# The first weight load of a two-branch decode kernel, cut into eight transfers by partition

## The chip, the cores and the metric

The kernel runs on one core of a Trainium2 chip; the other cores are idle. The metric is the device time of one execution in microseconds (us). Before the change three runs gave a median of 1324.18 us, with a lowest of 1323.75 and a highest of 1324.31.

## The reference

Two attention branches, A and B, work on the same input and are mixed by a gate. Each branch projects the input to one query per head and batch entry, scores it against a cached key tensor, takes the softmax and applies it to a cached value tensor, then projects the result out.

```python
# B=2 batch entries, Sq=1, D=512; Hq=Hkv=32 heads, Sk=4096 tokens, Dh=128; all float32
def branch(x, k_cache, v_cache, wq, wo):
    q = (x @ wq).reshape(B, Sq, Hq, Dh).transpose(0, 2, 1, 3)
    scores = einsum("bhqd,bhkd->bhqk", q, k_cache) * (Dh ** -0.5)
    p = softmax(scores, axis=-1)
    o = einsum("bhqk,bhkd->bhqd", p, v_cache)
    return o.transpose(0, 2, 1, 3).reshape(B, Sq, Hq * Dh) @ wo

g = sigmoid((A_x * gate_w).sum(-1, keepdims=True))
result = g * branch(A_x, ...A...) + (1 - g) * branch(A_x, ...B...)
```

Each cache is 2 x 32 x 4096 x 128 floats, 134 MB; there are four of them, and four weight matrices of 8.4 MB each. All of it is read once: 570.43 MB.

## The kernel before

The work is cut into 32 units: branch, group of four heads, batch entry. A unit has a key tile and a value tile of 128 partitions x 16384 floats, that is 64 KB on each partition and 8.39 MB in all (8192 KB). On-chip memory has room for three such tiles: two for keys (`kt[0]`, `kt[1]`) and one (`vt`) that holds the values, and ahead of them the query weights of the branches, one after the other.

All large loads are issued by SyncE (SP in the profile) on one queue, in the order of the code. That order is: A's query weights into `vt` (`load_wq("A")`, L218 to L221), unit 0's keys into `kt[0]` in two halves (L225), B's query weights into `vt` (L486), unit 1's keys into `kt[1]`, unit 0's values into `vt`, and from there keys and values of the following units in turn (L508 to L512), then the two output weights. A load that overwrites a tile waits on SyncE until the tile's last reader is done: B's query weights wait for `queries("A")`, the values wait for the matmuls that read the values before (`v_free`), the keys wait for VectorE's scores of two units ago (`k_free`).

At the start TensorE turns the input into columns (`cols`, L287 to L289). It then runs `projections()` (L327), a loop of two rounds, one for each branch, whose body is written once: take 16 from the semaphore `wq_landed`, which the weight load raises by 16 when it has landed; take one from `cleared`, which VectorE raises when it has zeroed the accumulators `qa`; then 64 matmuls of the 512 x 4096 weights. `take` (L94) waits for a semaphore and lowers it again, so that both rounds can wait for the same count. `queries(n)` (L341) then has ScalarE copy the sums into `vt` and VectorE transpose them into `qcol`; when VectorE's last reading of `vt` is done, SyncE may issue the next load of `vt`.

The weights lie on the partitions as rows of the matrix: partition p holds the four rows 4p to 4p+3, which are 64 KB in a row in memory on either side.

From there VectorE multiplies every key tile with the queries and sums it up (L392 and L395, the scores), ScalarE takes the exponentials, and TensorE multiplies them with the values (L371). At the end the sums of all units are projected out.

## Time and profile before

| | |
|---|---|
| median of the runs | 1324.18 us (1323.75 to 1324.31) |
| profiled execution: span from first to last instruction | 1322.3 us |
| bytes read | 570.43 MB |
| VectorE busy | 1165.3 us |
| TensorE busy | 331.7 us |
| ScalarE busy | 100.7 us |
| issue of A's query weights on SyncE | 0.96 us after the span's start, 0.40 us long |
| issue to landing of that load | 21.8 us |
| first projection's matmuls on TensorE | from 23.06 us, 9.49 us long |

The profiled execution's own time is its span of 1322.3 us; it has no other clock, and the runs stand 1.9 us above it. In the profile an engine's name with a q behind it is that engine's sequencer (SPq is SyncE's, which issues loads). A stretch of the trace is given as start and end in us from the span's start, with the busy time of every engine in it, how many instructions, the clock granted to TensorE (PEclk), the share of the 16 DMA engines' time that packets took, and the bytes moved per second. Both of the last are booked at the moment in which a packet begins, so that a short stretch can show more than its share.

### The profile page before, as it was taken

Reading aid. Unit: us, or ns where it says so; the run is one execution under the profiler, and the core shown is the slowest. Engines: PE = TensorE matmul, PEld = TensorE weight load, DVE = VectorE, ACT = ScalarE, POOL = GpSimd, SP = SyncE. Lnnn points to the kernel's source line nnn. Section 1 sums busy time; section 2 is a strip of 40 time slices with the busy share of each in tenths; the row PEclk is TensorE's granted clock in tenths of the full one; section 3 lists DMA queues with packets and bytes.
Section 4 is the critical chain, followed back from the end, with each engine's and each line's share of the span. In section 5 each row is a group of like instructions: output and inputs, shape, how many; then the busy total and the mean of one; then the engine's idle time right before and its main releaser. Section 6 shows DMA issues by size and latency. Waiting matters only on the chain. (4 is left out here: it accounts for less than half of the span.)

```text
span 1322.3 us, 6216 instructions
## 1 busy us (share of the span) xinstructions
PE 331.7 (25%) x2382; PEld 90.3 (7%) x2382; DVE 1165.3 (88%) x316; ACT 100.7 (8%) x328; POOL 0.7 (0%) x6
## 2 busy tenths in 40 slices
PE   3112222211222221122222122222212322311256
PEld 0000000000000000000000000000000000000011
DVE  1978999999999999999999999999999999999961
ACT  0000100001010000101000010100001010000100
POOL 0000000000000000000000000000000000000000
PEclk9566666556666655666665666666556666555678
DMA  9999999999999999999999999999999999999998
GB/s 404 453 412 443 442 416 442 442 416 442 442 418 442 440 436 424 442 440 418 442 440 418 442 442 416 442 442 424 436 442 436 422 442 440 418 442 442 417 442 352
DMA packets 10820, 570.51 MB, mean 431 GB/s; under 512 B 1207, under 2 KB 1467, under 8 KB 1726
## 3 DMA queue, kind: packets, MB, share of 16 engines
q1 hardware_dynamic: 10804, 570.43, 99.6%
q8 instruction: 3, 0.05, 0.0%
q14 instruction: 3, 0.02, 0.0%
q10 hardware_dynamic: 10, 0.01, 0.0%
HBM read 570.43 MB, written 0.00 MB: 431 GB/s over the span
## 5 line engine op out<-in xcount | busy, mean ns | idle before, releaser
L392 DVE TENSOR_TENSOR kt<-kt,q 128x16384 f32<-128x16384 f32 x31 | 534.0, 17226 | 71.3 <-DVEq L97 71.3
L395 DVE TENSOR_REDUCE sc<-kt 128x128 f32<-128x16384 f32 x31 | 533.8, 17220 | 1.1
L371 PE MATMUL vp<-vt,pr 128*32 128x512 f32 x1984 | 283.1, 734 | 915.5 <-PEq L97 915.5
L371 PEld LDWEIGHTS vp<-vt,pr 128*32 128x32 f32 x1984 | 77.9, 132 | 1120.7 <-issue 1120.7
L367 ACT ACTIVATE pr<-sc,nm 32x128 f32<-32x128 f32 x128 | 50.9, 398 | 108.1 <-ACTq L97 102.8
L430 ACT ACTIVATE pr<-nil 128x512 f32<-128x512 f32 x31 | 19.3, 623 | 456.8 <-ACTq L97 456.8
L451 ACT ACTIVATE vs<-vp,slot 128x128 f32 x15 | 5.5, 368 | 448.1 <-ACTq L97 448.1
L337 PE MATMUL qa<-vt,cols 128*2 128x512 f32 x128 | 18.4, 739 | 39.9 <-PEq L97 39.9
L367 ACT ACTIVATION_READ_ACCUMULATOR pr<-sc,nm (+1 forms) x128 | 23.5, 184 | 0.0
L416 DVE SCALAR_TENSOR_TENSOR vs<-vp,slot,vs 128x128 f32 x45 | 15.8, 351 | 8.6 <-DVEq L97 7.6
L599 DVE COPY kt<-qa 2x128 f32<-2x128 f32 x1 | 0.3, 278 | 23.8 <-PE qa L481 23.8
L352 DVE STREAM_TRANSPOSE vt<-vt 128x1024 f32<-128x1024 f32 x2 | 2.4, 1224 | 17.1 <-ACT vt L348 17.1
L498 DVE TENSOR_REDUCE sc<-kt 128x64 f32<-128x8192 f32 x2 | 17.4, 8686 | 0.1
L496 DVE TENSOR_TENSOR kt<-kt,q 128x8192 f32<-128x8192 f32 x2 | 17.4, 8688 | 0.0
L455 ACT ACTIVATE vp<-nil 128x512 f32<-128x512 f32 x15 | 9.0, 600 | 99.2 <-ACTq L97 99.2
L544 DVE SCALAR_TENSOR_TENSOR vs<-vp,slot,vs 128x128 f32<-128x128 f32 x3 | 1.1, 351 | 12.9 <-ACT vs L542 12.8
L371 PE MATMUL vp<-kt,pr 128*32 128x512 f32 x64 | 9.0, 724 | 10.9 <-DMA kt<-in_B_v_cache_dram 10.9
L466 PE MATMUL most<-vt,kt 128*2 128x512 f32 x64 | 9.6, 765 | 6.5 <-DMA vt<-in_A_wo_dram 6.5
L400 DVE TENSOR_REDUCE rm<-sc 128x1 f32<-128x128 f32 x31 | 8.7, 281 | 2.3
L406 DVE STREAM_TRANSPOSE q<-qsel 128x128 f32<-128x128 f32 x30 | 9.3, 311 | 1.0
L289 DVE COPY cols<-bank 128x8 f32<-128x8 f32 x1 | 0.2, 167 | 10.0 <-PE bank L287 10.0
L401 DVE STREAM_TRANSPOSE across<-rm 128x32 f32<-128x32 f32 x31 | 6.6, 212 | 1.1
(73 smaller groups left out, 60.4 us busy)
## 6 DMA issues: line engine op xcount, KB each, us to landing
kt<-in_A_k_cache_dram SPq DMA_DIRECT2D x2, 4096.0 KB, 35.6
kt<-in_B_wo_dram SPq DMA_DIRECT2D x1, 4096.0 KB, 33.1
kt<-in_B_wo_dram SPq DMA_DIRECT2D x1, 2048.0 KB, 37.6
kt<-in_B_wo_dram SPq DMA_DIRECT2D x1, 1024.0 KB, 39.5
kt<-in_B_wo_dram SPq DMA_DIRECT2D x1, 512.0 KB, 40.3
vt<-in_A_v_cache_dram SPq DMA_DIRECT2D x16, 28.5
kt<-in_B_k_cache_dram SPq DMA_DIRECT2D x16, 42.6
kt<-in_B_wo_dram SPq DMA_DIRECT2D x1, 256.0 KB, 40.4
```

Of the source, the lines that this page charges most:

```text
L337: last = nc.tensor.matmul(t[h * QT:h * QT + B], cols[:, c], blocks[:, c, i, h], start=c == 0, stop=c == KC - 1)
L367: do(lambda x: x.activation(padded[h, :, b, j * VC:(j + 1) * VC], s[h].rearrange("p (c a) -> p c a", a=VC), AF.Exp, bias=m[h], accum_out=l ...
L371: return x.matmul(vp[c % STRIPS * QT:(c % STRIPS + 1) * QT], padded[:, c].rearrange("p b m -> p (b m)"), t[:, c * VC:(c + 1) * VC].rearran ...
L392: at = D_.do(lambda x: x.tensor_tensor(kt[o], kt[o], q[:, None, :].to_broadcast([P, NS, DH]), op=ALU.mult), after)
L395: at = D_.do(lambda x: x.tensor_reduce(sc[o], kt[o], axis=AX.X, op=ALU.add), at)
L406: return D_.do(lambda x: x.transpose(q, qsel[:, 0].to_broadcast([P, DH // QT, QT])), at)
L416: at = D_.do(lambda x: x.scalar_tensor_tensor(vs[:, g], vp[:, a * DH:(a + 1) * DH], slot[:, a:a + 1], vs[:, g], op0=ALU.mult, op1=ALU.add) ...
L430: return A_.do(lambda x: x.activation(padded[:, :, b], nil[:, :, None].to_broadcast([P, NVC, G * VC]), AF.Copy))
L455: A_.do(lambda x: x.activation(vp, nil.to_broadcast([P, VC * DH]), AF.Copy))
L466: put("pe", lambda x: x.matmul(most[s * QT:s * QT + B], on[:, k, r], wo[n][:, r], start=n == "A" and r < STRIPS, stop=n == "B" and r >= EA ...
L496: put("dve", lambda x: x.tensor_tensor(t, t, q[:, None, :].to_broadcast([P, NS // 2, DH]), op=ALU.mult), [r_q], [r])
L498: put("dve", lambda x: x.tensor_reduce(sc[0][:, h * NS // 2:(h + 1) * NS // 2], t, axis=AX.X, op=ALU.add), [r], [R()])
```

## The change

A's query weights go out as eight transfers instead of one. Transfer r holds the partitions r, r+8, r+16 and so on to r+120: 16 partitions of 64 KB, 1 MB in all. The first seven raise a new semaphore, `wq_first`, and the last one raises `wq_landed`. TensorE waits for 7 x 16 on `wq_first` once, ahead of the loop over the branches; inside the loop it takes 16 from `wq_landed` as before. B's query weights still go out as one transfer.

```diff
+EACH = 8
...
+        wq_first = sem("wq_first")
...
         def load_wq(n):
             S.before("sp", [], [r_vt])
-            nc.sync.dma_start(vt.rearrange("p r d -> p (r d)"),
-                              ins[n + "_wq"].rearrange("(p c) f -> p (c f)", c=KC)).then_inc(wq_landed, 16)
+            to, src = vt.rearrange("p r d -> p (r d)"), ins[n + "_wq"].rearrange("(p c) f -> p (c f)", c=KC)
+            if n == "B":
+                nc.sync.dma_start(to, src).then_inc(wq_landed, 16)
+                return
+            for r in range(EACH):
+                nc.sync.dma_start(to[r::EACH], src[r::EACH]).then_inc(wq_first if r < EACH - 1 else wq_landed, 16)
...
         def projections():
-            S.wait("pe", r_cols.writers)
+            S.wait("pe", [*r_cols.writers, (wq_first, 16 * (EACH - 1))])
```

On SyncE, at the start of the program, the loads stood like this before (a row names the line, the tile that is written, the tensor that is read, and the shape; what it waits for stands in brackets):

```order
L220 DMA vt<-in_A_wq_dram 128x16384
L106 DMA kt_85<-in_A_k_cache_dram 128x8192 x2
L106 UNCONDITIONAL_BRANCH
L220 DMA vt<-in_B_wq_dram 128x16384 [waits done_dve]
L231 DMA kt_86<-in_A_k_cache_dram 128x16384 [waits landed_x,done_pool,landed_y,done_act,done_pe]
```

and now like this:

```order
L227 DMA vt<-in_A_wq_dram 16x16384 x8
L107 DMA kt_85<-in_A_k_cache_dram 128x8192 x2
L107 UNCONDITIONAL_BRANCH
L224 DMA vt<-in_B_wq_dram 128x16384 [waits done_dve]
L237 DMA kt_86<-in_A_k_cache_dram 128x16384 [waits landed_x,done_pool,landed_y,done_act,done_pe]
```

One row has become eight, ahead of the two halves of unit 0's keys; what follows is as it was. On TensorE, around the start of the projections, the program now reads:

```order
L293 MATMUL bank<-kt_86 128x3 [waits landed_y,landed_x,done_pool]
L293 MATMUL bank<-kt_86 128x3 x3
L310 MATMUL bank<-kt_86 128x2 [waits done_dve]
L335 UNCONDITIONAL_BRANCH [waits wq_first]
L343 MATMUL qa_89<-vt,cols 2x512 [waits wq_landed,cleared]
```

The wait for `wq_first` stands at the loop's entry, where there was none; the matmuls behind it waited for `wq_landed` and `cleared` before as well.

## The prediction

> **What bounds the kernel now.** I read the page's summary first, for who is busy and what was moved.

> ```profile
> span 1322.3 us, 6216 instructions
> PE 331.7 (25%) x2382; PEld 90.3 (7%) x2382; DVE 1165.3 (88%) x316; ACT 100.7 (8%) x328; POOL 0.7 (0%) x6
> DMA  9999999999999999999999999999999999999998
> q1 hardware_dynamic: 10804, 570.43, 99.6%
> ```

> VectorE is busy for 88% and would be the suspect, but the DMA row shows 9 from the first slice on, and the queue that SyncE feeds (q1) fills 99.6% of the time of 16 DMA engines. Then stretches of the trace, each of 19.3 us at first, then two long ones:

> ```profile
> core 0: us, PE busy (x) PEld busy (x) DVE busy (x) ACT busy (x) POOL busy (x), PEclk, DMA share, GB/s
> 5.00:21.80 16.80, 1.20 (x6) 1.05 (x6) 4.91 (x19) 0.17 (x1) 0.00 (x0) 1.00 1.01 437
> 21.80:41.10 19.30, 9.49 (x64) 1.76 (x64) 6.85 (x7) 1.08 (x2) 0.00 (x0) 0.84 1.01 435
> 41.10:60.40 19.30, 0.00 (x0) 0.00 (x0) 19.27 (x3) 0.00 (x0) 0.00 (x0) 0.50 1.00 435
> 60.40:79.70 19.30, 8.90 (x64) 1.68 (x64) 13.83 (x9) 3.04 (x10) 0.00 (x0) 0.77 1.00 435
> 99.00:699.00 600.00, 144.09 (x1024) 39.72 (x1024) 558.25 (x135) 46.28 (x152) 0.00 (x0) 0.62 1.00 435
> 699.00:1279.00 580.00, 139.00 (x960) 38.17 (x960) 539.80 (x125) 46.65 (x157) 0.00 (x0) 0.61 1.00 434
> ```

> The rate is the same 434 to 437 GB/s everywhere, with VectorE idle or full, TensorE idle or at work. A load of 8.39 MB takes 8.39 / 0.435 = 19.3 us, and loads follow one another with no gap. So the kernel is one stream of loads; the chain of waits confirms its end:

> ```profile
> 1276.98 39.55 DMA kt<-in_B_wo_dram
> 1316.53 0.04 issue
> ```

> The last load ends at 1316.5 us, and 5.8 us of matmuls and storing follow. The stream has no idle time that could swallow a delay: **what A's query weights cost more or less in the stream moves the end by the same amount**, as long as the next loads are queued in time. The sums below are made on the span of 1322.3 us; the median of the runs, 1324.18, is 1.9 us above it, and I carry that over.

> **How one load looks now.** Packets are booked when they begin, so thin stretches show them as rounds:

> ```profile
> 1.80:2.60 0.80, 0.00 (x0) 0.00 (x0) 0.00 (x0) 0.80 (x1) 0.00 (x0) 1.00 3.88 1316
> 2.60:5.00 2.40, 0.00 (x0) 0.00 (x0) 0.00 (x0) 0.46 (x1) 0.00 (x0) 1.00 0.00 0
> 5.00:5.60 0.60, 0.00 (x0) 0.00 (x0) 0.00 (x0) 0.00 (x0) 0.00 (x0) 1.00 4.03 1748
> 5.60:7.40 1.80, 0.00 (x0) 0.00 (x0) 0.00 (x0) 0.00 (x0) 0.00 (x0) 1.00 0.00 0
> 7.40:8.00 0.60, 0.00 (x0) 0.00 (x0) 0.00 (x0) 0.00 (x0) 0.00 (x0) 1.00 4.04 1751
> ```

> Each busy stretch is one round of A's weights: 1748 GB/s x 0.60 us = 1.05 MB, sixteen packets of 64 KB, one partition's row for each DMA engine. The rounds begin at 5.0 and 7.4: 2.4 us a round (19.3 / 8 = 2.41), eight rounds for the load. The first takes longer: it begins at 1.8 to 2.6 and the second at 5.0, about 3.0 us, so the start costs about 0.6 us once.

> **The change, part by part.** *The same bytes in the same number of packets:* eight transfers of sixteen rows of 64 KB are again eight rounds of sixteen packets, if each of the 16 engines takes one row of each transfer. *More issues:* SyncE's part of the time line is

> ```profile
> 0.96 0.40 SPq L220 DMA_DIRECT2D vt<-in_A_wq_dram  x1
> 1.41 0.89 SPq L106 DMA_DIRECT2D kt<-in_A_k_cache_dram  x2
> 35.34 0.33 SPq L220 DMA_DIRECT2D vt<-in_B_wq_dram  x1
> 35.86 0.33 SPq L231 DMA_DIRECT2D kt<-in_A_k_cache_dram  x1
> 74.47 0.33 SPq L239 DMA_DIRECT2D vt<-in_A_v_cache_dram  x1
> ```

> At 0.44 us each (0.89 / 2), seven more end 3.1 us later, and unit 0's keys are issued by about 5.4 us instead of 2.3. The engines then still have most of A's weights to move (till 21.8), and a transfer of one round lasts 2.4 us against an issue of 0.44: nothing runs dry. Cost nothing, covered by the queue; without that cover it would be 3.1 us. *Seven more completion marks on each engine:* the key load that goes out in two halves ran at 435 GB/s (21.80 to 41.10), as did the undivided one after it, so one mark more is under the resolution of 0.1 us; seven are under 0.7, and I take 0.1. *The wait for `wq_first`:* behind it on TensorE stand only the projections, which need the whole of the weights anyway. It ends with the seventh transfer, ahead of the eighth or with it: nothing.

> *Where the rows land.* This is the term that decides. Between 5.0 and 21.8 us each engine moves 64 KB in 2.4 us, 27 GB/s, and sixteen make the 435 that no stretch exceeds. A ceiling that stays the same whatever the compute engines do is a fixed width of the path: either of the 16 movers, or of the entrances by which they write into on-chip memory. The trace holds only loads over all 128 partitions, so no row tells which. If it is the movers, it doesn't matter which partitions a transfer holds. If it is the entrances, a transfer over all partitions must be dealt out so that each mover has an entrance to itself, since it reaches the full rate; a transfer of every eighth partition leaves no such choice. All sixteen rows in flight have the same place within a group of eight partitions, and all movers go on to the next place together, so they would keep meeting at some entrances while others stand empty, through all eight transfers.

> Bounds: below, the change wins back the slow start, 0.6 us for the long first round and 0.6 for the spread of the first starts, -1.2. Above, all sixteen rows through one entrance would be sixteen times 2.4 us a round, 8 x 15 x 2.41 = +289. The least sharing that there can be throughout is two movers to an entrance: a round then takes 2 x 2.41 and the load 8 x 2.41 = **19.3 us more**. I take that, the sharing nearest to the rows, with up to 0.6 us back, since the slow start overlaps with a slower round: +19.0.

> [...]

> *What is late next.* A's weights land around 42 us instead of 22.8 (0.96 + 21.8, below); every load behind them starts later by the same. The matmuls and the copies:

> ```profile
> vt<-in_A_wq_dram SPq DMA_DIRECT2D x1, 21.8
> 10.39 0.61 PE L287 MATMUL bank<-kt 3*128 3x3 f32 x4 [10.39 <-DMA kt<-in_gate_w_dram]
> 23.06 9.49 PE L337 MATMUL qa<-vt,cols 128*2 128x512 f32 x64 [10.68 <-PEq L97]
> 35.12 0.20 DVE L353 COPY qcol<-vt 128x64 f32<-128x64 f32 x1
> ```

> From landing to the issue of B's weights it is 35.34 - 22.8 = 12.5 us, and in that time unit 0's keys (19.3 us of stream) keep the engines busy until 41.1: 5.8 us to spare. Both shift together, so the spare time stays; the stream gets no hole, and nothing is caught up either. The small loads of the input and the gate, for which TensorE waits until 10.39, go through engines that also carry the weights and may come up to twice as late, near 20 us; the columns are needed at 42. Sum: 1322.3 + 19.0 = 1341.3 of span, 1324.2 + 19.0 = **1343.2 us**, 1.4% slower.

> **The rivals.**

> *The movers are the limit* (not slower). For it: the one rate in all rows, which fits this as well; every row that was read is of 128 partitions. Against it: nothing in the trace. Then the load stays at eight rounds of 2.41 us: 1324.2 + 0.1 for the marks, less up to 1.2 at the start, 1323.1 to 1324.3.

> *The change doesn't spread a transfer over all movers:* rows are dealt out by the partition they go to, so a transfer of every eighth partition uses half of the movers, two rows each; the first four transfers feed one half, the last four the other. Then the second half starts four issues later, 4 x 0.44 = 1.8 us, and each mover still carries eight rows: at most +1.8, 1326.0, within what can't be told. For it: full rate with 128 partitions needs some such order. Against it: the rows can't show it.

> *A faster start:* sixteen rows are prepared sooner than 128, so all movers begin at once. It can give the 1.2 us of the bound, 1323.0, which is no measurable gain; more than that isn't there to be had, because the stream has no other gap.

> *Sharing by four:* sixteen rows on four entrances, a round of 4 x 2.41: 8 x 3 x 2.41 = +57.8, 1382. Against it: distances of eight should reach more places than that.

> *Sharing only in part,* since the movers drift apart: half of the 19.3, 1334. Against it: the rounds above stay 2.4 us apart with starts inside 0.6 us, so the movers hardly drift.

> **How the numbers follow.** Less than 0.2% (2.6 us) can't be told from no change here. From the rows alone movers and entrances fit equally; I lean to the entrances because a rate that is the same to 1% in stretches with quite different reads, and with any load on the compute engines, is more easily a width of the memory's side. Chances: sharing by two 0.76, movers the limit 0.11, dealt by partition 0.06, sharing by four 0.03, in part 0.02, a start that wins over 2.6 us 0.02. Slower: 0.76 + 0.03 + 0.02 = 0.81; within 0.2%: 0.11 + 0.06 = 0.17; faster 0.02. The likeliest case's own range is 1341 (the start's 1.2 us won back, and a little drift) to 1347 (a tenth of 38.6 us lost where two streams meet). It holds about 0.7 by itself, so the range has to reach to the cases without a change: 1323 to 1347, which leaves out about 0.1.

> **What would show it.** Right: in stretches of the changed trace A's weights run at about 217 GB/s until about 41 us, with rounds 4.8 us apart; landing after the issue of the first transfer about 40 us; the first projection's matmuls begin near 42 us; B's weights are issued near 54.5; from there 435 GB/s in every stretch and the span 19 us longer; the matmuls and the scores as long as before. Wrong: rounds 2.4 us apart as now and the projection at about 23 us (the movers are the limit); half of the packets in the first rounds, the others 1.8 us later (dealt by partition); 110 GB/s (sharing by four). A hole in the stream between unit 0's keys and B's weights would make the step on the spare time wrong, and the sum would grow by the hole.

## The result, and the profile after

The changed kernel takes 1344.98 us (median; 1344.79 to 1345.37), the kernel before 1324.18: a ratio of 1.0158, with a 95% interval of 1.0147 to 1.0170. It is 20.8 us slower; the forecast was 19.0 us slower, 1343.2 us.

The page of the changed kernel, the lines that answer to those shown of before:

```profile
span 1343.1 us, 6223 instructions
PE 331.8 (25%) x2382; PEld 90.9 (7%) x2382; DVE 1165.2 (87%) x316; ACT 100.7 (8%) x328; POOL 0.7 (0%) x6
DMA  9899999999999999999999999999999999999998
GB/s 219 344 437 438 435 437 437 435 437 433 422 429 437 437 435 437 437 435 437 437 420 429 435 437 437 435 437 437 435 437 433 422 429 437 437 435 437 438 435 349
q1 hardware_dynamic: 10916, 570.43, 99.6%
```

The engines do the same work in the same time, the queue is as full as it was (99.6%), but in the first of 40 slices the DMA engines move 219 GB/s, with a busy share of 9 tenths. They are occupied and deliver half. The cause lies in the first 1.3 slices, where A's weights are loaded. There, in stretches that each hold the beginnings of one round of packets (up to 1.7 us behind the start of the stretch):

```profile
core 0: us, PE busy (x) PEld busy (x) DVE busy (x) ACT busy (x) POOL busy (x), PEclk, DMA share, GB/s
1.60:6.60 5.00, 0.00 (x0) 0.00 (x0) 0.00 (x0) 1.28 (x1) 0.08 (x1) 1.00 0.97 211
6.60:11.70 5.10, 1.20 (x6) 1.05 (x6) 1.81 (x8) 0.17 (x1) 0.00 (x0) 1.00 1.01 206
...
16.80:21.90 5.10, 0.00 (x0) 0.00 (x0) 0.00 (x0) 0.00 (x0) 0.00 (x0) 1.00 1.00 206
21.90:26.80 4.90, 0.00 (x0) 0.00 (x0) 0.00 (x0) 0.00 (x0) 0.00 (x0) 1.00 1.01 214
26.80:31.90 5.10, 0.00 (x0) 0.00 (x0) 0.00 (x0) 0.00 (x0) 0.00 (x0) 1.00 1.00 206
...
37.00:42.10 5.10, 0.00 (x0) 0.00 (x0) 0.00 (x0) 0.00 (x0) 0.00 (x0) 1.00 1.01 206
42.10:61.45 19.35, 8.83 (x64) 1.71 (x64) 6.36 (x7) 1.08 (x2) 0.00 (x0) 0.92 0.98 413
61.45:80.80 19.35, 0.00 (x0) 0.00 (x0) 19.32 (x3) 0.00 (x0) 0.00 (x0) 0.50 1.05 454
```

A round of sixteen 64 KB rows (206 GB/s x 5.10 us = 1.05 MB) takes 5.1 us where it took 2.4. One round, the fifth, takes 4.9. Unit 0's keys begin behind the eighth round, at 42.4 us, and their first round still overlaps the last slow packets, which end at 43.4. The mean of 413 and 454 GB/s in the last two stretches is the old rate within 0.4%: packets are booked when they begin, so what the one lacks the other has. Thin stretches show the first two rounds of the keys and the first of B's weights, before:

```profile
21.90:22.50 0.60, 0.00 (x0) 0.00 (x0) 0.00 (x0) 0.00 (x0) 0.00 (x0) 1.00 2.04 874
23.10:23.70 0.60, 0.60 (x4) 0.06 (x8) 0.00 (x0) 0.00 (x0) 0.00 (x0) 1.00 2.02 874
41.20:41.90 0.70, 0.00 (x0) 0.00 (x0) 0.70 (x1) 0.00 (x0) 0.00 (x0) 0.50 3.47 1498
```

and after:

```profile
42.40:43.50 1.10, 0.00 (x0) 0.00 (x0) 0.00 (x0) 0.00 (x0) 0.00 (x0) 1.00 1.52 477
44.30:44.90 0.60, 0.34 (x4) 0.14 (x8) 0.00 (x0) 0.00 (x0) 0.00 (x0) 1.00 2.02 874
62.50:63.00 0.50, 0.00 (x0) 0.00 (x0) 0.50 (x1) 0.00 (x0) 0.00 (x0) 0.50 4.85 2097
```

The trace has the start of every packet, and the mean of a round's sixteen starts tells how the delay grows (us):

| | before | after | later by |
|---|---|---|---|
| first round of A's weights | 2.20 | 2.61 | 0.4 |
| second round of A's weights | 5.26 | 7.46 | 2.2 |
| first round of unit 0's keys | 22.18 | 42.98 | 20.8 |
| second round of unit 0's keys | 23.38 | 44.63 | 21.2 |
| first round of B's weights | 41.54 | 62.78 | 21.2 |

What follows is shifted:

```profile
0.96 5.04 SPq L227 DMA_DIRECT2D vt<-in_A_wq_dram  x8
6.05 1.06 SPq L107 DMA_DIRECT2D kt<-in_A_k_cache_dram  x2
56.18 0.33 SPq L224 DMA_DIRECT2D vt<-in_B_wq_dram  x1
...
44.56 8.83 PE L343 MATMUL qa<-vt,cols 128*2 128x512 f32 x64 [33.74 <-PEq L98]
...
1297.91 39.43 DMA kt<-in_B_wo_dram
```

The last load ends 20.8 us later (1337.3 against 1316.5). That is 0.4 us less than the delay of B's weights in the table, which is within the 0.6 us by which single runs of either kernel differ; the 1280 us of stream between passed the delay on. B's weights are issued 20.8 us later too (56.18 against 35.34), but that is a coincidence: the first projection begins 21.5 us later (44.56 against 23.06) and in this profile is 0.7 us shorter (8.83 against 9.49).

### The profile page after: what moved, and what is told of

It is laid out like the page before. It is cut to its first block, busy times and chain, and to the rows that moved or that the text cites. A ratio compares the mean times of both kernels' runs of the same rounds, so it can differ in the third digit from the quotient of the medians.

```text
span 1343.1 us, 6223 instructions
## 1 busy us (share of the span) xinstructions
PE 331.8 (25%) x2382; PEld 90.9 (7%) x2382; DVE 1165.2 (87%) x316; ACT 100.7 (8%) x328; POOL 0.7 (0%) x6
## 2 busy tenths in 40 slices
DMA packets 10932, 570.51 MB, mean 425 GB/s; under 512 B 1319, under 2 KB 1579, under 8 KB 1838
## 3 DMA queue, kind: packets, MB, share of 16 engines
q1 hardware_dynamic: 10916, 570.43, 99.6%
HBM read 570.43 MB, written 0.00 MB: 425 GB/s over the span
## 5 line engine op out<-in xcount | busy, mean ns | idle before, releaser
L436 ACT ACTIVATE pr<-nil 128x512 f32<-128x512 f32 x31 | 19.3, 624 | 460.1 <-ACTq L98 460.1
L550 DVE SCALAR_TENSOR_TENSOR vs<-vp,slot,vs 128x128 f32<-128x128 f32 x3 | 1.1, 351 | 12.5 <-ACT vs L548 12.4
L343 PEld LDWEIGHTS qa<-vt,cols 128*2 128x2 f32 x128 | 3.4, 94 | 76.4 <-issue 76.4
```

The lines of the kernel that those rows point to most:

```text
L343: last = nc.tensor.matmul(t[h * QT:h * QT + B], cols[:, c], blocks[:, c, i, h], start=c == 0, stop=c == KC - 1)
L436: return A_.do(lambda x: x.activation(padded[:, :, b], nil[:, :, None].to_broadcast([P, NVC, G * VC]), AF.Copy))
```

## The experiments

All but the last vary only how A's weights are cut, in `load_wq`; the last cuts B's weights as well. The theory is that of the prediction: rows in flight together meet at a limited number of entrances into on-chip memory. The runs below test it by their own times; none shows an entrance. Where the text counts entrances, sixteen, eight or four, that is an estimate from the rates: 435 GB/s over all partitions, 206 in the change, 112 with sixteen neighbours, at one mover to an entrance in the first case.

### Eight transfers over all partitions

```diff
-                nc.sync.dma_start(to[r::EACH], src[r::EACH])...
+                at = slice(r * NS * DH // EACH, (r + 1) * NS * DH // EACH)
+                nc.sync.dma_start(to[:, at], src[:, at])...
```

> A's query weights go out as eight transfers again, but each over all 128 partitions with an eighth of the columns (8 KB of each row). The number of transfers, the bytes and TensorE's waits are those of the change; only the partitions that are in flight together differ. Theory (sixteen rows that lie eight partitions apart share eight entrances into on-chip memory, two by two): no sharing, the load at about 435 GB/s, 1324 us, within 0.3% of the kernel before. Rival 'eight transfers cost more than one' (issue, marks, small transfers): as the change, about 1345 us.

Measured: 1324.30 us against 1324.06 of before, ratio 1.0002 (0.9992 to 1.0011). Eight transfers as such cost nothing that these runs can tell. Their issue takes a little longer than I had reckoned (0.50 us each against 0.44), and the queue covers it:

```profile
0.96 4.03 SPq L228 DMA_DIRECT2D vt<-in_A_wq_dram  x8
5.03 0.98 SPq L107 DMA_DIRECT2D kt<-in_A_k_cache_dram  x2
```

### Sixteen neighbours in each transfer

```diff
-                nc.sync.dma_start(to[r::EACH], src[r::EACH])...
+                at = slice(r * P // EACH, (r + 1) * P // EACH)
+                nc.sync.dma_start(to[at], src[at])...
```

> Eight transfers of sixteen neighbouring partitions each (0 to 15, 16 to 31, ...), instead of every eighth; all else as in the change. [...] Rival 'the cost comes from reading rows that lie 512 KB apart': neighbouring rows are 64 KB apart, no loss, 1324 us. Rival 'eight transfers cost more than one': 1345 us, as the change.

Measured: 1379.17 us against 1324.06, ratio 1.0417 (1.0399 to 1.0434), +55.1 us. Two of its rounds, in stretches of its own trace:

```profile
19.15:28.51 9.36, 0.00 (x0) 0.00 (x0) 0.33 (x1) 0.00 (x0) 0.00 (x0) 1.00 1.00 112
28.51:37.88 9.37, 0.00 (x0) 0.00 (x0) 0.00 (x0) 0.00 (x0) 0.00 (x0) 1.00 1.00 112
```

With the same number of transfers and other partitions in each, the load falls from 206 to 112 GB/s, as it would with fewer entrances. The figures were missed: I expected 1382 to 1387 us and at least four times a round of before, 4 x 2.42 = 9.7 us, where the four was an assumption that no run had shown, and 9.37 is 3.87 times. So, if the entrances are four, a shared one is not held to the 2.42 us per row that a mover takes alone: 112 / 4 = 28.0 GB/s an entrance, as an estimate, against 435 / 16 = 27.2 GB/s a mover. Where two meet it is less, 206 / 8 = 25.7, if the entrances are eight.

### Reading and writing taken apart

The next two kernels put the rows of the weights on other partitions than the reference's; they compute queries from permuted weights, with the same amount of work.

```diff
+                at = slice(r * P // EACH, (r + 1) * P // EACH)
-                nc.sync.dma_start(to[r::EACH], src[r::EACH])...
+                nc.sync.dma_start(to[r::EACH], src[at])...      # the first of the two
+                nc.sync.dma_start(to[at], src[r::EACH])...      # the second
```

> The reading side and the writing side are taken apart: transfer r reads sixteen neighbouring rows (16r to 16r+15) and writes them to every eighth partition (r, r+8, ...), so the weight rows stand on other partitions than the reference's and the queries are those of permuted weights; the work is the same in amount. Theory (the writing side decides): as the change, 1345 us, rounds of 5.1 us. Rival (the reading side decides): as the kernel before, 1324 us.

Measured: 1344.97 us, ratio 1.0160 (1.0143 to 1.0176). It is the change's time (1344.98), with neighbouring rows read. Its rounds are as long as the change's, the short one too:

```profile
16.78:21.88 5.10, 0.00 (x0) 0.00 (x0) 0.00 (x0) 0.00 (x0) 0.00 (x0) 1.00 1.00 206
21.88:26.78 4.90, 0.00 (x0) 0.00 (x0) 0.00 (x0) 0.00 (x0) 0.00 (x0) 1.00 1.01 214
```

> The reverse: transfer r reads every eighth row (r, r+8, ...) and writes them to sixteen neighbouring partitions (16r to 16r+15); again the weight rows are permuted and the amount of work is the same. [...] Rival (the reading side decides): as the change, 1345 us.

Measured: 1378.18 us, ratio 1.0412 (1.0394 to 1.0429), with rounds of the blocks' length:

```profile
28.30:37.55 9.25, 0.00 (x0) 0.00 (x0) 0.00 (x0) 0.00 (x0) 0.00 (x0) 1.00 1.00 113
```

The absolute time missed my range, 1382 to 1387 us as for the blocks, for the same reason. The verdict stands on the pair: **which partitions are written decides**, and which rows are read hardly matters (1 us of 55).

### Two halves, every fourth, every second

The slice of the first, with two transfers, is that of the blocks with `EACH = 2`; the others are the change with `EACH = 4` and `EACH = 2`.

> A's query weights go out as two transfers: partitions 0 to 63 and 64 to 127. Theory, with two facts of its form open: sixteen movers on one half of the partitions; if a half reaches only half of the entrances, sharing by two throughout, 1343 to 1346 us although there are only two transfers. If a half reaches all entrances, 1324 us. Rival 'the cost is per transfer': a quarter of the change's 20.8 us at most (two transfers for eight), below 1330 us.

Measured: 1345.30 us (median), ratio 1.0191 (1.0143 to 1.0239), the interval being wide because of one run of 1357.59; the other three lie between 1344.97 and 1345.41. Two transfers of 4 MB cost what eight of 1 MB did:

```profile
17.18:22.31 5.13, 0.00 (x0) 0.00 (x0) 2.61 (x10) 0.00 (x0) 0.00 (x0) 1.00 1.00 204
```

So a half, 64 partitions, is held to 204 GB/s, by the theory because it reaches only eight entrances, and its rows are dealt out over all sixteen movers: a round is sixteen packets (204 GB/s x 5.13 us = 1.05 MB), and the movers' share is 1.00. Were rows given to a mover by their partition, the two halves would have run side by side at the full rate.

> Four transfers of every fourth partition (32 partitions, 2 MB each). [...] If the movers take neighbouring rows of a transfer one after the other (mover 0 the rows at 0 and 4, mover 1 those at 8 and 12), then sixteen rows eight apart are in flight together, as in the change: 1345 us. If rows are dealt out so that a transfer that covers all entrances uses all of them at once, 1324 us. Rival 'the cost is per transfer': half of the change's, 1334 us.

> Two transfers of every second partition (64 partitions, 4 MB each). As with every fourth: if the movers take neighbouring rows of a transfer in turn (mover 0 those at 0, 2, 4, 6), sixteen rows eight apart are in flight and the time is 1345 us; if the dealing spreads them over all entrances, 1324 us. Rival 'the cost is per transfer': a quarter of the change's at most, below 1330 us.

Measured: 1324.44 us for every fourth and 1324.28 for every second, both 1.0002 (0.9992 to 1.0012) against 1324.05 of before. With every second partition:

```profile
5.00:21.80 16.80, 1.20 (x6) 1.05 (x6) 4.92 (x19) 0.17 (x1) 0.00 (x0) 1.00 1.01 437
```

A transfer needn't hold all partitions for the full rate, 437 GB/s here. By the theory it reaches all entrances evenly, and its rows are dealt out so that the sixteen in flight spread over them; the runs show the rate alone. Taking neighbouring rows in turn is ruled out, since that would have put the change's sixteen rows in flight, with rounds of 5.1 us. By the theory, giving the rows to movers 0 to 15 in order and starting over is ruled out too: the first sixteen rows of every fourth partition would be those of partitions 0 to 60, which lie in one half, and a half gave rounds of 5.1 us. Which rule deals them is open: no run shows the mover of a row.

### Quarters of 32 neighbours

The slice is that of the blocks with `EACH = 4`.

> A's query weights in four transfers of 32 neighbouring partitions (0 to 31, 32 to 63, ...). [...]

Measured: 1344.86 us (median), ratio 1.0186 (1.0137 to 1.0236), again with one run apart at 1357.44 and three between 1344.58 and 1344.98. Rounds of it:

```profile
11.37:16.48 5.11, 1.19 (x6) 1.05 (x6) 1.92 (x8) 0.17 (x1) 0.00 (x0) 1.00 1.01 206
16.48:21.61 5.13, 0.00 (x0) 0.00 (x0) 2.99 (x12) 0.00 (x0) 0.00 (x0) 1.00 1.00 204
```

I expected 1345 us, as with the halves; if the time went by the number of neighbours, it would lie near 1360, an estimate between the rounds of 16 and of 64. 32 neighbours are as fast as 64 (5.11 and 5.13 us a round against 5.13), and not between 16 (9.37 us) and 64: from 32 to 64 the number of neighbours makes no difference. The rounds of this study's cuts by partition take 2.4 us, 4.9 to 5.13 or 9.25 to 9.37, which fits one, two or four movers to an entrance; no run shows more of it than these times. Two and four times 2.41 us would be 4.82 and 9.64, as an estimate; measured are 5.10 and 9.37, and the measurement decides.

### The change in another order

```diff
-            for r in range(EACH):
+            for k in range(EACH):
+                r = k // 2 + k % 2 * EACH // 2
```

> The change with its eight transfers in another order: 0, 4, 1, 5, 2, 6, 3, 7 instead of 0 to 7. Theory (two rows of the transfer in flight meet at each of eight entrances, the first four transfers at one set of entrances, the last four at the other): the order doesn't undo the sharing, 1343.5 to 1345 us. An open point of the changed kernel's trace is told apart: one round of eight, the fifth, in which the transfers go over to the other set, took 4.91 us and the others 5.10. If a change of set makes a round shorter, all rounds behind the first take 4.91 here, 1.1 us less in all (six rounds more at -0.19): about 1343.8 us. If the fifth place or those rows do it, one round is short as before: 1345 us. Rival 'movers drift apart and use both sets at once': rounds towards 2.4 us, well below 1340 us.

Measured: 1348.61 us as a median of runs that don't agree: 1343.45, 1343.79, 1353.44 and 1353.47; ratio 1.0171 (1.0133 to 1.0209). The profile is that of a long one. In the weights' load all rounds behind the first are now short, as these show:

```profile
6.75:11.65 4.90, 1.20 (x6) 1.05 (x6) 2.08 (x9) 0.17 (x1) 0.00 (x0) 1.00 1.01 214
11.65:16.56 4.91, 0.00 (x0) 0.00 (x0) 2.83 (x11) 0.00 (x0) 0.00 (x0) 1.00 1.00 214
...
26.36:31.28 4.92, 0.00 (x0) 0.00 (x0) 0.00 (x0) 0.00 (x0) 0.00 (x0) 1.00 1.00 213
41.10:131.00 89.90, 20.26 (x136) 3.93 (x140) 63.36 (x19) 4.00 (x12) 0.00 (x0) 0.64 1.01 389
131.00:251.00 120.00, 30.34 (x212) 8.38 (x208) 107.47 (x25) 8.62 (x29) 0.00 (x0) 0.60 1.00 434
```

The short fifth round of the change, 4.90 us, goes with the passage from the transfers 0 to 3 to the transfers 4 to 7, which this order makes between any two that follow each other; that it is a passage to another set of entrances is the theory, as expected. The two shorter runs, 1343.45 and 1343.79, lie near the 1343.8 us that follows from it. The loads that come after the weights explain the profiled run's length: for 90 us they move 389 GB/s with the movers fully occupied (share 1.01), then 434 again. The same stretch of the change reads

```profile
41.10:131.00 89.90, 26.79 (x192) 6.04 (x192) 68.78 (x19) 4.13 (x12) 0.00 (x0) 0.68 1.00 431
```

so 89.9 x (1 - 389 / 431) = 8.8 us are lost there, of the 9.8 by which the long runs exceed the short ones. At that rate a round of sixteen 64 KB rows takes 1.05 MB / 389 GB/s = 2.70 us instead of 2.42, as an estimate. From 62 to 132 us the rate is 392 GB/s, from 135 to 255 us 436. What starts and ends the stretch isn't settled.

### Both branches' weights

```diff
-            if n == "B":
-                nc.sync.dma_start(to, src).then_inc(wq_landed, 16)
-                return
...
-                nc.sync.dma_start(to[r::EACH], src[r::EACH]).then_inc(wq_first if r < EACH - 1 else wq_landed, 16)
+                nc.sync.dma_start(to[r::EACH], src[r::EACH]).then_inc(wq_landed, 16)
...
-            S.wait("pe", [*r_cols.writers, (wq_first, 16 * (EACH - 1))])
+            S.wait("pe", r_cols.writers)
...
-                take("pe", wq_landed, 16)
+                take("pe", wq_landed, 16 * EACH)
```

All eight transfers of a branch raise `wq_landed` here, and TensorE takes 8 x 16 from it in each round.

> Branch B's query weights go out in eight transfers of every eighth partition as well. Theory (the stream of loads has no slack at all, and a slower load anywhere in it moves the end by its whole loss): the change's 20.8 us twice, 1365 to 1367 us. Rival (the loss shows only at the start, where nothing else is queued; later loads have slack or the movers are no longer in step): 1345 to 1355 us.

Measured: 1366.34 us, ratio 1.0319 (1.0301 to 1.0336), +42.0 us: twice 21.0. B's load runs in the middle of the stream, behind other loads, and loses the same (eight rounds of 1.05 MB begin in the first of these stretches, so 221 GB/s):

```profile
62.00:100.00 38.00, 0.00 (x0) 0.00 (x0) 32.54 (x9) 0.00 (x0) 0.00 (x0) 0.50 1.07 221
101.00:701.00 600.00, 145.49 (x1024) 39.44 (x1024) 541.08 (x127) 45.75 (x151) 0.00 (x0) 0.62 1.00 433
```

The loss isn't one of the start, and the stream has no slack in which to hide it.

## Why the prediction was right, point by point

**The stream of loads sets the end, and passes a delay on whole.** Right. B's weights came 21.2 us later and the last load 20.8, and a second loss of the same kind added a second 21 us.

**The movers share entrances two by two.** Right as far as the times tell: the partitions written decide (reading and writing taken apart: 1344.97 us with every eighth written, 1378.18 with neighbours), the number of transfers doesn't (eight over all partitions: 1324.30), and sixteen neighbours make it worse, 9.37 us a round against 5.10. I had no row for this, and chose the least sharing possible: as far as the rows of before go, that it was by two was luck. No run shows two movers at one entrance, or an entrance at all; what the runs showed in its place are rounds of 5.10 us at 206 GB/s, where they took 2.42 at 435.

**The size, 19.3 us less the start's 0.3.** This is the term that was mis-sized, 19.0 against 20.8. A shared round takes 5.1 us and not twice 2.41 = 4.82: 206 GB/s is 5% below half of 435. By the table above, the seven rounds from the second on add 20.8 - 2.2 = 18.6 us, where doubling would add 16.9: 1.7 of the miss is here. I had allowed for such a loss only in the upper end of the range, "a tenth of 38.6 us lost where two streams meet". The passage to unit 0's keys adds another 0.4 (20.8 to 21.2), for which the sum had no term. The start gave back 0.2, since the second round begins 2.2 us later and not 2.41. Two things make this up: the first round is only 1.8 us longer than before, 0.6 back as the bound had it, but it begins 0.4 us later, which the sum didn't have. So 19.3 - 0.2 + 1.7 + 0.4 = 21.2, and the end of the profile, 20.8 later, is that within the difference of single runs.

**More issues, marks, the wait for `wq_first`: nothing.** Right as far as it can be told, by the eight transfers over all partitions at +0.2 us within an interval that holds zero. My price for an issue was low: 5.04 us for eight of the change's is 0.63 each, not 0.44; the cover of the queue is what counted. The queue's packets rose from 10804 to 10916, by 112 = 7 x 16, and those under 512 B by the same 112 (1207 to 1319), which fits one mark more on each mover for each further transfer. The 0.1 us that I set down for the marks isn't in the sum of 19.0, and no run tells so small a time.

**What is late next.** Right in kind: B's weights are issued at 56.18 us (forecast near 54.5), 6.3 us before their first packets begin at 62.5, against 5.9 before (35.34 and 41.2 to 41.3), and no hole opens. The landing and the projection were put at 42 us. The projection begins at 44.56, since the load was longer and its last packets end only when the last movers go over to the keys, by 43.5 us. The small loads of the input and the gate, which I let come up to twice as late, came sooner: TensorE's first matmuls begin at 8.83 us,

```profile
8.83 0.61 PE L293 MATMUL bank<-kt 3*128 3x3 f32 x4 [8.83 <-DMA kt<-in_gate_w_dram]
```

against 10.39 before. That step was wrong and cost nothing.

**The rivals.** "The movers are the limit" falls with the change itself. "Dealt by partition" falls with the two halves, which ran one behind the other on all sixteen movers (share 1.00, 204 GB/s). "Sharing by four" has its time in sixteen neighbours, 9.37 us a round and 112 GB/s, not in distances of eight, 5.10 us and 206 GB/s. "Sharing in part" falls with the rounds of 5.1 us; only the fifth round, the first of the transfers 4 to 7, is 0.2 us shorter (4.90). "A faster start" isn't there: the first round begins 0.4 us later than before.

## What to carry to other kernels

In a kernel that is one unbroken stream of loads, look at what each transfer has in flight at a time and where it lands: the busy share stayed at 99.6% while the rate of this load halved, so the bytes per second of a stretch tell what the share hides. Cut over the columns, or by every second or fourth partition, this load cost nothing that could be told (1324.30, 1324.28 and 1324.44 us); halves, quarters and every eighth partition doubled its time (rounds of 5.1 us instead of 2.4), and sixteen neighbours made it nearly four times as long (9.37 us). Where a load has to be cut, those first cuts are the ones to try. A trace that holds only loads of one shape can't tell a limit of the movers from one of the place they write to, and one run with the same rows read and other partitions written does.
